# Retention attention and routed experts on one core: larger first pieces, constants by head pair, second buffers for two tiles

## The chip, the cores and the metric

The kernel runs on one core of a Trainium2 chip. The metric is device time in microseconds (us), the median of three runs. One further execution was profiled; every row below comes from it.

## The reference

```python
def _attn_ref(q, k, v):              # (8, 8, 576, 64) each
    scores = scale * np.matmul(q, k.transpose(0, 1, 3, 2))
    gamma = 1.0 - 2.0 ** (-5.0 - np.arange(H))
    Dmat = np.where(rel >= 0, gamma[:, None, None] ** rel, 0.0)
    return np.matmul(scores * Dmat, v)

def _moe_ref(x, w_gate, w1, w2):     # x: (4608, 512), 8 experts
    logits = x @ w_gate
    order = np.argsort(-logits.flatten())
    # greedy in this order: each token takes one expert,
    # each expert at most 576 tokens
    ...
    out[mask] = np.maximum(x[mask] @ w1[e], 0.0) @ w2[e]
```

The output of the attention, put together over heads, is the x of the expert part.

## The kernel before

The work has three parts, one behind the other: attention (to about 170 us), the routing search, and eight experts with a first layer (`ph`) and a second (`py`). The change touches attention alone.

Attention runs over 16 units. A unit `u` is a pair of batch entries with a pair of heads (`hp = u % 4`), and has nine blocks of 128 tokens. Four inputs are loaded per unit: `kin` and `qin` (transposed k and q, 1152 columns of fp32 on 128 partitions), `vin` (v by tokens, 1152) and `nin` (k by tokens, 1024). One block is numbered `g = 9*u + blk`. Its steps are these.

- `A(g)`: scores of the block on PE, two heads, into `pA` (line 588). Behind each fourth block VectorE multiplies by the decay mask and leaves `am` (line 593).
- `kscale2`: GpSimd (POOL) scales `nin` with constants into `ks` (line 568).
- `ST(u, c)`: the running state of k and v on PE into `pS` (line 605), which ScalarE scales into `S` (line 611).
- `XS` and `XW`: the block's output on PE, from the state (lines 628 and 630) and from `am` (line 640), into `pX`, a PSUM tile with two buffers. VectorE scales it into `xT` (line 652), which frees the `pX` buffer.
- `rows(bp, blk)`: VectorE transposes finished blocks of `xT` into `xr` (line 693). After every third block four DMAs write `xr` to DRAM as `xd` (line 698). `xr` has one buffer, so the first transpose of the next group waits until these writes are done.

Each engine works through its instructions in program order. All loads stand in one queue, that of SyncE (SP), in program order as well: a load whose buffer is still in use holds back every load behind it. `kin`, `qin` and `vin` have three buffers each, `nin` one. Loads of unit `u + 2` are issued while unit `u` runs (`ahead`).

The first two units are loaded in pieces. `fetch` takes a string: a lower-case letter with a number is a piece of unit 0, an upper-case one of unit 1; `c` and `h0`, `h1` are the constants. Before, unit 0 has three pieces per input (256, 256 and the remaining columns) and unit 1 two. The 3664 columns of constants lie by kind (`m1`, `m2`, `ex`, `ks`, `ss`), so that those of one head pair come in three transfers (line 532).

`warm(n)` issues n matmuls of a constant bf16 tile `full` into a PSUM tile that nothing reads. Before, it is called in the later parts only.

Of the kernel before, what the change touches and what calls it, by code (L numbers as in the profile page):

```python
# [10 lines left out]
F32 = mybir.dt.float32  # L11
F32R = mybir.dt.float32r
BF16 = mybir.dt.bfloat16
I32 = mybir.dt.int32
ALU = mybir.AluOpType
# [4 lines left out]
NP, HP, NB = 4, 4, 9  # L20
# [3 lines left out]
def consts_np():  # L24
    h = np.arange(H); g = (1.0 - 2.0 ** (-5.0 - h)).astype(np.float64)
    k = np.arange(128)[:, None, None]; q = np.arange(128)[None, None, :]
    gm = g[None, :, None]
    m1 = np.where(k <= q, gm ** (-k), 0.0)
    km = k % 64
    m2 = np.where((k // 64 == q // 64) & (k <= q), gm ** (-km), 0.0)  # L30
    m1 = np.broadcast_to(m1, (128, 8, 128)); m2 = np.broadcast_to(m2, (128, 8, 128))

    p = np.arange(128); gh = g.reshape(HP, 2)[:, p // 64].T
    i = np.arange(128)
    e1 = 0.125 * gh[:, :, None] ** i
    e2 = 0.125 * gh[:, :, None] ** (i % 64)
    ss = gh[:, :, None] ** (128.0 * np.arange(1, 5))
    c = np.arange(4)
    ks = g.reshape(HP, 1, 1, 2)[None] ** (-(128.0 * c[None, None, :, None, None] + p[:, None, None, None, None]))
    ks = np.broadcast_to(ks, (128, HP, 4, 2, 2))  # L40
    f = lambda a: np.ascontiguousarray(a, dtype=np.float32).reshape(128, -1)
    return np.concatenate([f(m1), f(m2), f(np.stack([e1, e1, e2], axis=2)), f(ks), f(ss)], axis=1)

def layout(q, k, v):

# [36 lines left out]
class Route:  # L82
# [9 lines left out]
    def fetch(s, nc, fc_d):  # L92
        s.nc = nc
        s.fc = s.pool.tile([128, fc_d.shape[1]], F32, name="rc_f")
        nc.sync.dma_start(s.fc, fc_d)
# [411 lines left out]

def attention(tc, nc, P, qk, vk, cst_d, wg_d, rf, xd, Lg):
    cst = P['c'].tile([128, 2*1024+3*512+64+16], F32, name="cst", tag="xg")
    W0 = cst.shape[1]  # L510
    m1 = cst[:, 0:1024].rearrange("p (h q) -> p h q", h=8)
    m2 = cst[:, 1024:2048].rearrange("p (h q) -> p h q", h=8)
    ex = cst[:, 2048:3584].rearrange("p (h j q) -> p h j q", h=4, j=3)
    ks = cst[:, 3584:3648].rearrange("p (h q) -> p h q", h=4)
    ss = cst[:, 3648:3664].rearrange("p (h q) -> p h q", h=4)
    wg = P['a'].tile([128, HP, 32], F32, name="wg")
    LD = {}
    def load(u, what, cuts=None):

        bp, hp = divmod(u, HP)  # L520
        for i in what:
            n = 1024 if i == "n" else 1152
            t = P['ld'].tile([128, n], F32, name=i + "in", bufs=dict(q=3, k=3, v=3, n=1)[i])
            src = qk[bp, hp, "qk".index(i)] if i in "qk" else vk[bp, hp, :, :1152] if i == "v" else vk[bp, hp, :, 1152:]
            LD[u, i] = t
            if cuts:
                pieces[u, i] = [(t[:, a:b], src[:, a:b]) for a, b in zip((0,) + cuts, cuts + (n,))]
            else:
                nc.sync.dma_start(t, src)
# [2 lines left out]
    part = lambda a, b: nc.sync.dma_start(cst[:, a:b], cst_d[:, a:b])  # L532

    def consts(hp):
        for a, n in ((0, 256), (2048, 384), (1024, 256)):
            if a or hp:
                part(a + n*hp, a + n*hp + n)
    load(0, "kqvn", (256, 512))
    load(1, "kqvn", (512,))

    def fetch(order):
        for x in order.split():
            if x == "c":
                part(0, 256)
                part(3584, 3664)
            elif x[0] == "h":
                consts(int(x[1]))
            else:
                nc.sync.dma_start(*pieces[x[0].isupper(), x[0].lower()].pop(0))
    fetch("k0 q0 c v0 n0 k1 q1 h0 n1 v1 k2 q2 n2 v2")  # L550
    NS = 4
    Sb = []
    for i in range(NS):
# [13 lines left out]
    def kscale2(u, a, b):  # L567
        nc.gpsimd.tensor_tensor(KS[u][:, a:b], LD[u, 'n'].rearrange("p (a d) -> p a d", d=64)[:, a:b],  # L568
                                ks[:, u % HP, a:b, None].to_broadcast([128, b-a, 64]), op=ALU.mult)
# [3 lines left out]
    def A(g):  # L573
        if g >= G: return
        u, blk = divmod(g, NB); hp = u % HP
        if blk == 0 and 2 <= u + 1 < 16:
            if u < 3:
                consts(u + 1)
            if u == 2:
                R.fetch(nc, rf)  # L580
                nc.sync.dma_start(wg[:, :, 0:8], wg_d.rearrange("(hp p) e -> p hp e", p=128))

        n, j, tail = (4, blk % 4, "") if blk < 8 else (1, 0, "t")
        if j == 0: PA[0] = [P['ps'].tile([128, n, 128], F32, name=f"pA{h}" + tail, tag="y" if tail else "h0", bufs=2) for h in range(2)]
        s = slice(blk*128, blk*128+128)
        for h in range(2):
            r = slice(64*h, 64*h+64)
            nc.tensor.matmul(PA[0][h][:, j], LD[u, 'k'][r, s], LD[u, 'q'][r, s], start=True, stop=True, skip_group_check=True)  # L588
        if j == n - 1:
            m = m2 if tail else m1  # L590
            for h in range(2):
                am = P['w'].tile([128, n, 128], F32, name=f"am{h}" + tail, bufs=2)
                nc.vector.tensor_tensor(am, PA[0][h], m[:, None, 2*hp+h, :].to_broadcast([128, n, 128]), op=ALU.mult)  # L593
                for i in range(n): AM[g-j+i, h] = am[:, i]
    def ST(u, c):

# [91 lines left out]
    def rows(bp, blk):  # L688

        j = blk % 3  # L690
        if j == 0:
            TR[0] = P['w'].tile([128, 12, HP, 32], F32, name="xr", bufs=1)
        nc.vector.transpose(TR[0][:, 4*j:4*j+4].rearrange("p b h i -> p h b i"),  # L693
                            XT[bp][:, :, blk*128:(blk+1)*128].rearrange("p h (b i) -> p h b i", i=32))
        if j == 2:
            o = (bp*NB + blk - 2)*128
            for a in range(4):
                nc.sync.dma_start(xd[o:o+384, 128*a:128*a+128].rearrange("(b j) c -> j b c", j=32),
                                  TR[0][32*a:32*a+32].rearrange("p b h i -> p b (h i)"))
# [70 lines left out]
        for n, (i, a, b) in enumerate(((1, 0, 1), (1, 1, 2), (2, 0, 2), (3, 0, 2), (4, 0, 2))):  # L770
            at(g0+24+2*n, R.first_table, i, 2*bp+a, 2*bp+b)
    kscale(0)
    kscale2(0, 0, 4)
    A(0)
    A(1)
    ST(0, 0)
    kscale2(0, 4, 8)
    kscale2(0, 8, 16)
    nc.gpsimd.memset(wg, 0.0)
    fetch("K0 Q0 N0 V0 h1 K1 Q1 N1 V1")  # L780
    A(2)
    A(3)

    def ahead(g):

# [306 lines left out]
def build(tc, nc, qk, vk, cst, wg, rf, w1, w2, out):  # L1092
    with ExitStack() as top:
        P = {}
        P['c'] = top.enter_context(tc.tile_pool(name="c", bufs=1))
        P['ps'] = top.enter_context(tc.tile_pool(name="ps", bufs=1, space=bass.MemoryType.PSUM))
        dr = top.enter_context(tc.tile_pool(name="dr", bufs=1, space=bass.MemoryType.DRAM))
        top.enter_context(tc.manual_schedule())
        xd = dr.tile([N, DM], F32, name="xd")
        it = P['c'].tile([128, 128], I32, name="it")  # L1100
        nc.gpsimd.iota(it, pattern=[[1, 128]], base=0, channel_multiplier=-1)
        P['ident_r'] = P['c'].tile([128, 128], F32R, name="ident")
        nc.vector.tensor_scalar(P['ident_r'], it, 0.0, None, op0=ALU.is_equal)
        P['ident'] = P['ident_r'].bitcast(F32)
        Lg = P['c'].tile([128, 36, 8], F32, name="Lg")
        mix = Mixer()
        full = P['c'].tile([128, 512], BF16, name="full")
        nc.vector.memset(full, 1.0)

        def warm(n):  # L1110

            ps = P['ps'].tile([128, DM], F32, name="warm", tag="y", bufs=2)
            for _ in range(n):
                nc.tensor.matmul(ps, full[:, :128], full, start=True, stop=True)
        P['warm'] = warm
        with ExitStack() as ctx:
            Q = dict(P)
            for name, bufs in (("a", 1), ("ld", 2), ("w", 2), ("xt", 2)):
                Q[name] = ctx.enter_context(tc.tile_pool(name="a_" + name, bufs=bufs))
            R, rows = attention(tc, nc, Q, qk, vk, cst, wg, rf, xd, Lg)  # L1120

            def idle(what):

                if what not in ("row", "rows"):
                    warm(what)
                    return
                for _ in range(1 + (what == "rows")):
                    if rows:
                        rows.pop(0)()
                    else:  # L1130
                        warm(1)
            R.idle = idle
            run = moe(tc, nc, P, R, xd, w1, w2, out, mix)
            mix.drain(lambda: 0 in run.regs)
            while rows:
                rows.pop(0)()
        P['w'] = top.enter_context(tc.tile_pool(name="w", bufs=1))
        run()
# [18 lines left out]
```

## Time and profile before

| what | us |
|---|---|
| median of three runs (lowest, highest) | 676.65 (674.9, 677.34) |
| the profiled execution | 674.55 |
| its span, first to last instruction | 672.8 |
| PE busy in the span | 632.0 (94%) |
| VectorE (DVE) busy | 422.3 (63%) |
| GpSimd (POOL) busy | 180.7 (27%) |

Busy shares are averages over three parts with different limits. What holds a part up is read from the waits and the chain of that part. Times within a trace count from the first instruction.

### The profile page before, as it was taken

The page shows a single profiled execution, that of the slowest core. Times are in us where ns is not written, and L with a number is a line of the kernel's source. Part 1 is how long each engine was busy: PE and PEld are TensorE (multiplying, and loading weights), DVE is VectorE, ACT ScalarE, POOL GpSimd, SP SyncE. Part 2 cuts the span into 40 slices and gives each one's busy share as a digit, 9 for nine tenths or more (in the row PEclk, how much of TensorE's full clock was granted, in tenths as well). Part 3 has the DMA queues.
Part 4 walks back from the last instruction along what each step waited for, and adds up shares of the span by engine and source line. Part 5 has one row for each costly group of instructions (what it writes and reads, how often), then busy time and mean ns, then how long its engine had stood idle before and what let it go on. Part 6 is the DMA issues. An engine that isn't in the chain of part 4 may idle for free.

```text
span 672.8 us, 14118 instructions
## 1 busy us (share of the span) xinstructions
PE 632.0 (94%) x5376; PEld 543.3 (81%) x5376; DVE 422.3 (63%) x1603; ACT 273.6 (41%) x488; POOL 180.7 (27%) x234
## 2 busy tenths in 40 slices
PE   4999999897987999999999999999999999999995
PEld 3887788776756887797798799889889989988984
DVE  2477878777775797798799599679776302211200
ACT  1333333232325524655257245515724643652611
POOL 2222212212212106315214323315224134131111
PEclk9999999899998999999999999999999999999998
DMA  7997999993455946978859938947894895894421
GB/s 225 340 362 251 285 306 307 257 282 91 126 198 137 227 96 203 258 192 199 247 130 230 243 81 215 245 145 172 210 245 118 177 268 177 194 237 137 94 63 39
DMA packets 53427, 134.72 MB, mean 200 GB/s; under 512 B 6128, under 2 KB 22512, under 8 KB 53360
## 3 DMA queue, kind: packets, MB, share of 16 engines
q1 hardware_dynamic: 38400, 81.91, 37.1%
q0 software_dynamic: 14960, 51.91, 35.1%
q8 instruction: 42, 0.69, 0.4%
q14 instruction: 25, 0.20, 0.1%
HBM read 81.90 MB, written 18.87 MB: 150 GB/s over the span
## 4 chain that ended last, share of the span: by engine, by line
PE 63%; DVE 12%; issue 9%; DMA 8%; POOL 3%; ACT 3%; SPq 2%; POOLq 0%; DVEq 0%; ACTq 0%
PE py L1037 21%; PE ph L998 21%; PE pX L640 4%; PE pA L588 3%; PE pX L630 3%; PE pS L605 3%; DMA w2l<-raw 2%; DMA raw<-in_w 1%; POOL xg L953 1%; DMA qin<-in_qk 1%; PE pt L969 1%; PE r L340 1%; DMA xd<-xr 1%; PE pT L669 1%; DVE xr L693 1%
## 5 line engine op out<-in xcount | busy, mean ns | idle before, releaser
L1037 PE MATMUL py<-w2h,hb 128*128 128x512 f32 x576 | 188.3, 399 | 0.0
L998 PE MATMUL ph<-xh,w1h 128*128 128x320 f32 (+1 forms) x512 | 152.6, 302 | 2.5 <-ACT xh L971 1.7
L998 PE MATMUL ph<-xh,w1l 128*128 128x320 f32 (+1 forms) x512 | 150.0, 297 | 0.0
L998 PE MATMUL ph<-xl,w1h 128*128 128x320 f32 (+1 forms) x512 | 149.9, 297 | 0.0
L1037 PE MATMUL py<-w2l,hb 128*128 128x512 f32 (+1 forms) x320 | 125.4, 392 | 0.1
L1037 PEld LDWEIGHTS py<-w2h,hb 128*128 128x128 f32 x576 | 104.0, 188 | 20.7
L998 PEld LDWEIGHTS ph<-xh,w1h 128*128 128x128 f32 x512 | 96.7, 190 | 4.7 <-ACT xh L971 2.8
L998 PEld LDWEIGHTS ph<-xl,w1h 128*128 128x128 f32 x512 | 96.9, 191 | 0.5 <-DVE cs L344 0.3
L998 PEld LDWEIGHTS ph<-xh,w1l 128*128 128x128 f32 x512 | 96.7, 191 | 0.2 <-DMA w1l<-raw 0.2
L1005 DVE SCALAR_TENSOR_TENSOR hb<-ph,hb 128x256 fp32r<-128x256 f32 (+1 forms) x192 | 58.9, 351 | 56.9 <-ACT hb L1002 56.2
L1002 ACT ACTIVATE hb<-ph 128x256 fp32r<-128x256 f32 (+1 forms) x128 | 52.2, 409 | 102.1 <-PE ph L998 102.1
L611 ACT ACTIVATE S<-pS,cst 64x128 f32<-64x128 f32 x128 | 46.4, 363 | 108.1 <-PE pS L605 106.5
L1014 POOL DMA_INDIRECT out_y<-yt,idx x40 | 40.8, 1021 | 118.8 <-ACT yt L1054 76.6
L1037 PEld LDWEIGHTS py<-w2l,hb 128*128 128x128 f32 (+1 forms) x320 | 56.7, 177 | 13.7 <-DMA w2l<-raw 1.0
L568 POOL TENSOR_TENSOR ks<-nin,cst 128x512 f32<-128x512 f32 (+1 forms) x33 | 33.3, 1028 | 120.8 <-DMA nin<-in_vk 100.9
L1054 ACT ACTIVATE yt<-py 128x512 f32<-128x512 f32 x32 | 19.2, 599 | 105.1 <-PE py L1037 78.9
L942 POOL DMA_DIRECT2D w2l<-raw x32 | 28.8, 901 | 119.2 <-ACT hb L1002 119.2
L593 DVE TENSOR_TENSOR am<-pA,cst 128x512 f32<-128x512 f32 x64 | 41.0, 682 | 27.9 <-PE pA L588 21.8
L953 POOL DMA_INDIRECT xg<-xd,idx x40 | 40.7, 1017 | 51.6 <-issue 26.6
L1057 DVE TENSOR_TENSOR yt<-yt,py 64x512 f32<-64x512 f32 x8 | 5.4, 678 | 69.6 <-ACT yt L1056 69.4
L588 PE MATMUL pA<-qin,kin 64*128 64x128 f32 x512 | 39.5, 295 | 8.6 <-DMA qin<-in_qk 8.6
L588 PEld LDWEIGHTS pA<-qin,kin 64*128 64x128 f32 x512 | 33.0, 196 | 12.8 <-issue 8.0
(190 smaller groups left out, 967.8 us busy)
## 6 DMA issues: line engine op xcount, KB each, us to landing
raw<-in_w SPq DMA_DIRECT2D x64, 512.0 KB, 5.3
w2l<-raw POOLq DMA_DIRECT2D x32, 512.0 KB, 5.7
w1l<-raw POOLq DMA_DIRECT2D x31, 512.0 KB, 7.7
kin<-in_qk SPq DMA_DIRECT2D x14, 576.0 KB, 6.3
qin<-in_qk SPq DMA_DIRECT2D x14, 576.0 KB, 7.1
vin<-in_vk SPq DMA_DIRECT2D x14, 576.0 KB, 7.9
nin<-in_vk SPq DMA_DIRECT2D x14, 512.0 KB, 5.8
xd<-xr SPq DMA_DIRECT2D x36, 192.0 KB, 3.6
```

The lines of the kernel that those rows point to most:

```text
L568: nc.gpsimd.tensor_tensor(KS[u][:, a:b], LD[u, 'n'].rearrange("p (a d) -> p a d", d=64)[:, a:b], ks[:, u % HP, a:b, None].to_broadcast([12 ...
L588: nc.tensor.matmul(PA[0][h][:, j], LD[u, 'k'][r, s], LD[u, 'q'][r, s], start=True, stop=True, skip_group_check=True)
L593: nc.vector.tensor_tensor(am, PA[0][h], m[:, None, 2*hp+h, :].to_broadcast([128, n, 128]), op=ALU.mult)
L611: nc.scalar.activation(st[64*h:64*h+64, :, 64*h:64*h+64], PS[u][64*h:64*h+64], AF.Copy, scale=ss[64*h:64*h+64, hp, c:c+1])
L640: nc.tensor.matmul(px[64*h:64*h+64, :], v[:, blk*128+64*h:blk*128+64*h+64], AM[g, h], start=False, stop=blk < 8, skip_group_check=True)
L942: nc.gpsimd.dma_start(lo, raw, accum_op=ALU.add)
L953: nc.gpsimd.indirect_dma_start(out=xg[:n, j, :], out_offset=None, in_=xd[:, :], in_offset=bass.IndirectOffsetOnAxis(ap=found[e][:n, j:j+1] ...
L998: T.matmul(ps, w, x, start=(k == 0), stop=(k == 11))
L1002: A.activation(hb[:, f, c], ps, AF.Relu)
L1005: V.scalar_tensor_tensor(hb[:, f, to+a:to+b], ps[:, a:b], 0.0, hb[:, f, 256*s+a:256*s+b].bitcast(F32), op0=ALU.max, op1=ALU.subtract)
L1014: st = nc.gpsimd.indirect_dma_start(out=out[:, :], out_offset=bass.IndirectOffsetOnAxis(ap=found[e][:n, t:t+1], axis=0), in_=y[:n], in_off ...
L1037: T.matmul(ps[:m], a, w, start=(k == 0), stop=(k == last), skip_group_check=True)
```

## The change

Units 0 and 1 both come in two pieces of 512 and the remaining columns. The first piece of q is issued from ScalarE's queue, all the others from SP's. Constants lie by head pair, so that a pair needs one transfer. All pieces of units 0 and 1 stand in one string ahead of the computation; the second string, which stood behind the first `kscale2` calls, is gone. `nin` and `xr` have two buffers each. The program begins with seven matmuls on `full`; `A(0)` to `A(3)` stand ahead of `ST(0, 0)`, and the first `kscale2` covers eight parts and not four.

```diff
-    load(0, "kqvn", (256, 512))
+    load(0, "kqvn", (512,))
     load(1, "kqvn", (512,))
...
-            t = P['ld'].tile([128, n], F32, name=i + "in", bufs=dict(q=3, k=3, v=3, n=1)[i])
+            t = P['ld'].tile([128, n], F32, name=i + "in", bufs=dict(q=3, k=3, v=3, n=2)[i])
...
     def consts(hp):
-        for a, n in ((0, 256), (2048, 384), (1024, 256)):
-            if a or hp:
-                part(a + n*hp, a + n*hp + n)
+        part(80 + 896*hp + (0 if hp else 256), 976 + 896*hp)
...
             if x == "c":
-                part(0, 256)
-                part(3584, 3664)
+                part(0, 336)
             elif x[0] == "h":
                 consts(int(x[1]))
             else:
-                nc.sync.dma_start(*pieces[x[0].isupper(), x[0].lower()].pop(0))
-    fetch("k0 q0 c v0 n0 k1 q1 h0 n1 v1 k2 q2 n2 v2")
+                (nc.scalar if x == "q0" else nc.sync).dma_start(*pieces[x[0].isupper(), x[0].lower()].pop(0))
+    fetch("k0 q0 c n0 v0 k1 q1 h0 n1 v1 K0 Q0 h1 N0 V0 K1 Q1 N1 V1")
...
-            TR[0] = P['w'].tile([128, 12, HP, 32], F32, name="xr", bufs=1)
+            TR[0] = P['w'].tile([128, 12, HP, 32], F32, name="xr", bufs=2)
...
     kscale(0)
-    kscale2(0, 0, 4)
-    A(0)
-    A(1)
+    kscale2(0, 0, 8)
+    P['warm'](7)
+    for g in range(4):
+        A(g)
     ST(0, 0)
-    kscale2(0, 4, 8)
     kscale2(0, 8, 16)
     nc.gpsimd.memset(wg, 0.0)
-    fetch("K0 Q0 N0 V0 h1 K1 Q1 N1 V1")
-    A(2)
-    A(3)
...
+        full = P['c'].tile([128, 512], BF16, name="full")
+        nc.vector.memset(full, 1.0)
         it = P['c'].tile([128, 128], I32, name="it")
...
-        full = P['c'].tile([128, 512], BF16, name="full")
-        nc.vector.memset(full, 1.0)
```

SP's queue before, from the third pieces of unit 0 on. The names are the tiles above, the numbers are partitions by columns, and the bracket names what the issue waits for (`Pool` is GpSimd, `DMAHW` an earlier load).

```order
L549 DMA kin<-in_qk 128x640 [waits DMAHW4_49]
L549 DMA qin<-in_qk 128x640 [waits DMAHW5_49]
L549 DMA nin<-in_vk 128x512 [waits DMAHW6_49]
L549 DMA vin<-in_vk 128x640 [waits DMAHW7_49]
L549 DMA kin<-in_qk 128x512 [waits DMAHW0_49]
L549 DMA qin<-in_qk 128x512 [waits DMAHW1_49]
L549 DMA nin<-in_vk 128x512 [waits DMAHW6_49,DMAHW2_49,Pool_49]
L549 DMA vin<-in_vk 128x512 [waits DMAHW3_49]
L532 DMA cst<-in_cst 128x256 [waits DMAHW4_49]
```

The seventh of these is the first piece of `nin` for unit 1; it waits for GpSimd. The same place of the queue in the changed kernel, from the second pieces of unit 0's `nin` and `vin` on:

```order
L545 DMA nin<-in_vk 128x512 [waits DMAHW0_49]
L545 DMA vin<-in_vk 128x640 [waits DMAHW1_49]
L545 DMA kin<-in_qk 128x512 [waits DMAHW2_49]
L545 DMA qin<-in_qk 128x512 [waits DMAHW3_49]
L531 DMA cst<-in_cst 128x896 [waits DMAHW4_49]
L545 DMA nin<-in_vk 128x512 [waits DMAHW5_49]
L545 DMA vin<-in_vk 128x512 [waits DMAHW6_49]
```

Unit 1's `nin` no longer waits for GpSimd, and the constants of its head pair are one transfer ahead of it.

PE's first instructions before, behind the branch at the start (`pA` with a number is the buffer of one head):

```order
L588 MATMUL pA_122<-qin,kin 128x128
L588 MATMUL pA_123<-qin,kin 128x128
L588 MATMUL pA_122<-qin,kin 128x128
L588 MATMUL pA_123<-qin,kin 128x128
L605 MATMUL pS<-vin,ks 64x64 x4
L588 MATMUL pA_122<-qin,kin 128x128
L588 MATMUL pA_123<-qin,kin 128x128
```

In the changed kernel, from the last of the seven matmuls on `full`:

```order
L1107 MATMUL warm<-full 128x512
L584 MATMUL pA_133<-qin,kin 128x128
L584 MATMUL pA_134<-qin,kin 128x128
L584 MATMUL pA_133<-qin,kin 128x128
L584 MATMUL pA_134<-qin,kin 128x128
L584 MATMUL pA_133<-qin,kin 128x128
L584 MATMUL pA_134<-qin,kin 128x128
L584 MATMUL pA_133<-qin,kin 128x128
L584 MATMUL pA_134<-qin,kin 128x128
L601 MATMUL pS<-vin,ks 64x64 x4
```

Four blocks of scores now stand ahead of the first state product, where two stood.

## Rows read from the trace of the kernel before

**Rows 1.** The page: the chain that ended last, share of the span by engine
```profile
PE 63%; DVE 12%; issue 9%; DMA 8%; POOL 3%; ACT 3%; SPq 2%; POOLq 0%; DVEq 0%; ACTq 0%
```
**Rows 2.** Stretches: length, busy time (and count) by engine, PE clock, DMA share, GB/s
```profile
0.00:3.40 3.40, 0.00 (x0) 0.00 (x0) 1.05 (x2) 0.00 (x0) 1.43 (x9) 1.00 0.40 102
3.40:12.60 9.20, 3.15 (x24) 2.45 (x25) 1.29 (x2) 2.01 (x3) 1.23 (x2) 1.00 0.89 263
12.60:18.96 6.36, 6.34 (x56) 5.79 (x56) 2.24 (x5) 0.72 (x2) 2.23 (x3) 1.00 0.75 248
18.96:27.34 8.38, 8.30 (x122) 7.25 (x120) 4.64 (x9) 2.90 (x8) 1.04 (x1) 1.00 0.97 359
28.36:74.00 45.64, 44.98 (x635) 37.73 (x636) 30.81 (x94) 15.35 (x42) 10.22 (x10) 1.00 0.89 306
150.00:164.00 14.00, 9.95 (x138) 8.44 (x134) 10.51 (x33) 2.90 (x8) 4.08 (x5) 1.00 0.49 134
164.00:170.00 6.00, 5.77 (x65) 4.24 (x65) 4.89 (x12) 2.18 (x6) 0.00 (x0) 0.72 0.08 15
```
**Rows 3.** Waits of PE, 0 to 165 us: total, times, longest
```profile
PE pA L588 <- DMA qin<-in_qk: 8.6, 4, 3.6
PE pX L630 <- DVE xT L652: 6.8, 4, 2.8
PE pS L605 <- POOL ks L568: 1.9, 1, 1.9
```
**Rows 4.** The chain that ended last, 0 to 33 us: start, length, what
```profile
7.36 5.80 DMA nin<-in_vk
...
14.67 0.43 SPq L549
...
19.22 9.01 DMA qin<-in_qk
28.36 1.16 PE pA L588 x16
...
32.17 0.45 PE pS L605 x8
```
**Rows 5.** Waits of SP's queue, 0 to 36 us
```profile
SPq L549 <- DMA nin<-in_vk: 3.5, 1, 3.5
...
SPq L549 <- POOL wg L779: 1.2, 1, 1.2
```
**Rows 6.** DMA totals of 2 to 14, 14 to 16 and 20 to 28 us
```profile
DMA packets 2506, 3.20 MB, mean 267 GB/s; under 512 B 405, under 2 KB 1776, under 8 KB 2506
...
DMA packets 125, 0.23 MB, mean 117 GB/s; under 512 B 11, under 2 KB 11, under 8 KB 125
...
DMA packets 924, 2.92 MB, mean 365 GB/s; under 512 B 102, under 2 KB 102, under 8 KB 923
```
**Rows 7.** POOL in order of time, 5 to 15 us: start, length, instruction, wait
```profile
5.95 0.61 POOL L568 TENSOR_TENSOR ks<-nin,cst 128x256 f32<-128x256 f32 x1 [3.86 <-DMA nin<-in_vk]
...
13.23 1.04 POOL L568 TENSOR_TENSOR ks<-nin,cst 128x512 f32<-128x512 f32 x1 [3.56 <-DMA nin<-in_vk]
```
**Rows 8.** Tile kin, 0 to 36 us: ns min/median/max, first and last start
```profile
L588 PE MATMUL pA<-qin,kin x96: 272/272/579, 3.5 to 34.0; 64*128 64x128 f32 x96
```
**Rows 9.** VectorE in order of time, 140 to 172 us
```profile
150.55 0.71 DVE L693 STREAM_TRANSPOSE xr<-xT 128x512 f32<-128x512 f32 x1 [1.35 <-DMA xd<-xr]
...
162.68 0.71 DVE L693 STREAM_TRANSPOSE xr<-xT 128x512 f32<-128x512 f32 x1 [2.02 <-DMA xd<-xr]
```
**Rows 10.** PE in order of time, 140 to 172 us
```profile
140.82 0.71 PE L630 MATMUL pX<-qin,S 128*128 128x128 f32 x4
...
152.32 0.49 PE L630 MATMUL pX<-qin,S 128*128 128x128 f32 x2 [1.39 <-DVE xT L652]
...
164.22 0.49 PE L630 MATMUL pX<-qin,S 128*128 128x128 f32 x2 [2.75 <-DVE xT L652]
...
166.82 1.20 PE L630 MATMUL pX<-qin,S 128*128 128x128 f32 x4
```

More of the change, by code (lines that the diff above doesn't have):

```diff
@@ L41, in consts_np @@
     f = lambda a: np.ascontiguousarray(a, dtype=np.float32).reshape(128, -1)
-    return np.concatenate([f(m1), f(m2), f(np.stack([e1, e1, e2], axis=2)), f(ks), f(ss)], axis=1)
+    ex = np.stack([e1, e1, e2], axis=2)
+    return np.concatenate([f(ks), f(ss)] + [f(a) for p in range(HP) for a in (m1[:, 2*p:2*p+2], ex[:, p], m2[:, 2*p:2*p+2])], axis=1)
 def layout(q, k, v):
@@ L509, in attention @@
     cst = P['c'].tile([128, 2*1024+3*512+64+16], F32, name="cst", tag="xg")
[L510 to L515, printed above, removed]
+    ks = cst[:, 0:64].rearrange("p (h q) -> p h q", h=4)
+    ss = cst[:, 64:80].rearrange("p (h q) -> p h q", h=4)
+    cq = cst[:, 80:].rearrange("p (h j q) -> p h j q", h=4, j=7)
+    m1, ex, m2 = cq[:, :, 0:2], cq[:, :, 2:5], cq[:, :, 5:7]
     wg = P['a'].tile([128, HP, 32], F32, name="wg")
@@ L589, in A @@
         if j == n - 1:
-            m = m2 if tail else m1
+            m = (m2 if tail else m1)[:, hp]
             for h in range(2):
                 am = P['w'].tile([128, n, 128], F32, name=f"am{h}" + tail, bufs=2)
-                nc.vector.tensor_tensor(am, PA[0][h], m[:, None, 2*hp+h, :].to_broadcast([128, n, 128]), op=ALU.mult)
+                nc.vector.tensor_tensor(am, PA[0][h], m[:, None, h, :].to_broadcast([128, n, 128]), op=ALU.mult)
                 for i in range(n): AM[g-j+i, h] = am[:, i]
```

## Prediction

> **What bounds the kernel now.** I read the page first. PE has 63% of the chain that ended last and DMA 8% [rows 1], so the loads bind only somewhere. The table by stretch says where. PE is busy 3.15 of the 9.20 us to 12.60, and from 28.36 to 74 it is busy 44.98 of 45.64 us [rows 2]. The start waits, the middle does not.
>
> The waits name two things. PE waited 8.6 us for `qin` and 6.8 us for VectorE's `xT` up to 165 us [rows 3]. The chain shows the first as one path: a piece of `nin`, an issue on SP, the load of unit 2's q issued at 19.22 and landed 9.01 us later, and then PE's scores at 28.36 [rows 4]. Everything before 28.36 is set by how fast the first units arrive, with PE close behind: from 12.60 to 27.34 it is hardly idle [rows 2].
>
> The second is in VectorE's own order. Its transposes at 150.55 and 162.68 waited 1.35 and 2.02 us until the earlier `xr` had been written out [rows 9], and PE, whose `pX` buffers VectorE frees, stood 1.39 and 2.75 us [rows 10]. Those are 4.1 of the 6.8 us; the other two waits are shorter.
>
> **The change: the start.** What unit 2's scores need is the same before and after: units 0 and 1 at 2.294 MB each (three inputs of 1152 columns and one of 1024, 512 bytes a column) and 0.958 MB of constants, together 5.55 MB, then k and q of unit 2, 1.18 MB. I count at what rate they arrive.
>
> Up to 3.40 us the rate was 102 GB/s, 0.35 MB [rows 2]; at 267 GB/s that is 1.3 us, so the flow begins at 2.1. From 2 to 14 us it was 267 GB/s, when 1776 of 2506 packets were under 2 KB; from 20 to 28 us, with 102 of 924 under 2 KB, 365 GB/s [rows 6]. Between them there is a hole: SP stood 3.5 and 1.2 us for `nin` and what GpSimd did with it [rows 5], and from 14 to 16 us only 0.23 MB came in where 267 GB/s gives 0.53, which costs 0.30 / 0.267 = 1.1 us.
>
> Before by this count: 2.1 + 5.55/0.267 (20.8) + 1.18/0.365 (3.2) + 1.1 = 27.2. The trace has 28.2 (19.22 + 9.01) [rows 4]. The 1.0 us left over I keep as lag.
>
> After: the second `nin` buffer takes the hole away. Pieces are now 2 KB a row or more (512 columns and up; only `c` has 1344 bytes). Their rate lies between 267 and 365 GB/s; I take 300, nearer to the lower end because 2 KB is nearer to what ran there. That gives 2.1 + 18.5 + 3.2 + 1.0 = 24.8, which is 3.5 us before 28.36. Bounds: at 267 GB/s 27.1 (gain 1.2), at 365 GB/s 21.5 (gain 6.8).
>
> Next in line is unit 2's `nin`. The state product that needs it ran at 32.17 [rows 4], 3.81 us behind the scores. After, v and n, 1.11 MB at 365, land 3.05 us behind q, at 27.9, and GpSimd takes 1.04 [rows 7]: 28.9, where PE is there at 28.7. So 0.2 us are given back: **gain 3.3 us** (1.0 to 6.6).
>
> Can PE follow? Its work from 12.60 to 27.34 is 6.34 us in which the matmuls ran slowly, and 8.30 us. In the rows of `kin` one shape takes 272 ns and up to 579 [rows 8]; the long ones are those before 18.96, where the clock column reads 1.00 all the same. I read them as the lower level, 1.2 GHz, and what follows as 2.4. At 2.4 GHz the work is 6.34/2 + 8.30 = 11.5 us. After, the last piece of unit 0's q has landed when 1.88 MB are in, at about 9. With the same 6.4 us at the lower level PE is through at 9 + 6.4 + 8.3 = 23.7, a little ahead of 24.8.
>
> From 28.36 to 74 the loads flowed at 306 GB/s at a share of 0.89, and PE was idle for 0.66 of 45.64 us [rows 2]. The whole stretch moves forward, loads and PE alike; I cost that at nothing. If the loads don't move with it, it costs the 3.3.
>
> **Edits at nothing.** The seven matmuls on `full` run where PE had nothing (0 of the first 3.40 us [rows 2]). If they last longer than the first q takes, they delay scores whose state product waits for `ks` anyway. That product now needs eight parts scaled, 1.04 us and not 0.61 [rows 7]: 0.4 later, hidden since the next scores wait for q until 9. Eight constant transfers fewer save SP 8 × 0.43 us [rows 4], and q's first piece on ScalarE 0.43 more, but SP is ahead of the data, so nothing. The identity made 0.5 us later is used tens of us on.
>
> **The change: `xr`.** With two buffers a group's first transpose waits for the writes of the group before the last, long done. VectorE gets 1.35 + 2.02 = 3.4 us back, and PE's waits shrink by as much, from 4.1 to 0.8. Bounds: 4.1 if all of PE's wait goes; 2.0 if VectorE's own work ahead of `xT` keeps it late at the first place. **Gain 3.4 us.**
>
> Behind the second stall the granted clock was 0.72 in the mean from 164 to 170 us, a part of it at 1.2 GHz: four products took 1.20 us there and 0.71 at 140.82 [rows 2, 10]. PE had stood 2.75 us before. The loss is at most 0.28 × 6 = 1.7 us. With 0.8 us of standing left I expect it gone in the main; part of it VectorE would take up (4.89 busy of 6 us [rows 2]), so **gain 1.2 us** (0 to 1.7).
>
> **Sum.** 3.3 + 3.4 + 1.2 = 7.9 us. The profiled execution took 674.55 (span 672.8 and 1.75 around it), so it would be 666.7. It is 2.1 below the median of the runs; from 676.65 the same gain gives **668.7**.
>
> **The rivals.** *Larger pieces do not flow faster*, only the hole closes: the start gains 1.0, the total 1.0 + 4.6 = 5.6, 671.1. For it: at 12.60 to 18.96 mixed pieces ran no faster, 248 GB/s with the hole [rows 2]. Against it: 267 and 365 GB/s by packet size [rows 6]. The Trainium skill, DMA: Bandwidth & Descriptors, Specifications, says that a transfer reaches line rate from 512 B on; by that rule 1 KB rows lose nothing and this rival holds. The trace so far leans against it, though it can't part packet size from time.
>
> *The start's gain is given back*: PE, earlier by 3.3 us, meets loads of units 3 and 4 that are not earlier, because the flow is already at a share of 0.89 [rows 2]. Total 4.6, 672.0. Against it: those loads follow in the same queue, without the hole.
>
> *The `xr` wait is replaced*: the freed VectorE time ahead of `xT` goes into another wait of the same length, for `pX` or the scores. Only the start is left, 3.3 us, 673.3. Against it: nothing else is named in VectorE's wait at either place [rows 9].
>
> *Slower: PE's clock stays low.* The pieces come evenly and PE takes them in small bites with waits between, where before it had one long stretch from 12.60. My sum has 1.2 GHz until about 15.4. Each further us at it costs 0.5. All of the 7.9 is eaten after 15.8 us more, at 31; beyond 0.5% slower (another 3.4) it must last until 38, and until 40 it gives 676.65 + 12.3 - 7.9 = 681. Against it: once PE falls behind the loads it no longer waits, and before, 6.4 us of that sufficed [rows 2]. The Trainium skill, TensorE: Matmul & The Clock Gate, What's actually happening, says that the throttled level is the default and activity releases it; the long durations at the start agree [rows 8], and by that rule the seven first matmuls may bring the rise forward, which I don't count.
>
> **How the numbers follow.** About 0.5% (3.4 us) is what a measurement of this kernel can tell from no change. Forecast 0.55; larger pieces no faster 0.2; start given back 0.1; `xr` replaced 0.08; slower 0.05; 0.02 for more gain than the bounds. The forecast, larger pieces no faster, three quarters of the start given back, and the last are faster: 0.85. The other quarter and `xr` replaced are within 0.5%: 0.11. Slower 0.04, as a low clock can also end within the band. Bounds of the terms: 1.0 + 2.0 + 0 = 3.0 to 6.6 + 4.1 + 1.7 = 12.4, 673.6 to 664.3. The range 664 to 673 leaves out the slower case, most of the `xr` rival and what lies beyond the bounds.
>
> **What would show it.** Right: unit 2's scores begin at 24 to 26 us, SP issues unit 1's `nin` without GpSimd, the flow from 2 to 14 us is near 300 GB/s with no hole, VectorE has no wait for `xd<-xr`, PE's waits for `xT` sum to about 3.5 us, and the clock stays at 1.00 behind the last of them. Wrong: a flow of 267 (first rival), new waits for `qin` between 28 and 74 us (second), 1.39 and 2.75 us still there (third), or scores at 579 ns past 20 us (the slower one).

## The result, and the profile after

The changed kernel took 667.34 us (median of 4 runs, 665.16 to 667.43), the kernel before 676.43 beside it (4 runs, 674.9 to 677.34). The ratio is 0.986, with an interval of 0.9833 to 0.9887, so the gain is 9.1 us by the medians. The profiled execution took 667.28 us, its span is 665.5. Line numbers of the changed kernel are 4 lower than those of before in attention (`pA` is line 584, `pX` 626, `xr` 689).

The page, chain that ended last, share of the span by engine. The DMA share fell from 8% [rows 1] to 6%:

```profile
PE 66%; DVE 13%; issue 10%; DMA 6%; ACT 2%; POOL 2%; SPq 0%; POOLq 0%; DVEq 0%; ACTq 0%
```

The chain from 0 to 30 us (start, length, what) and the DMA totals of 2 to 14 and of 20 to 28 us:

```profile
0.75 3.50 DMA qin<-in_qk
...
6.37 6.78 DMA cst<-in_cst
...
13.17 8.81 DMA qin<-in_qk
...
22.11 1.16 PE pA L584 x16
...
24.36 0.41 PE pS L601 x8
...
24.85 1.05 POOL ks L564
...
25.95 0.45 PE pS L601 x8
```

```profile
DMA packets 2236, 4.50 MB, mean 375 GB/s; under 512 B 242, under 2 KB 370, under 8 KB 2236
...
DMA packets 849, 3.27 MB, mean 408 GB/s; under 512 B 95, under 2 KB 95, under 8 KB 848
```

Unit 2's scores begin at 22.11 instead of 28.36, and its state product at 25.95 instead of 32.17 [rows 4]. The load of unit 2's q takes as long as before (8.81 and 9.01 us), but it is issued at 13.17 instead of 19.22. The flow was 375 GB/s where it had been 267, and 408 where it had been 365 [rows 6].

PE's waits up to 165 us (total, times, longest), and the stretches (length, busy time and count of PE, PEld, VectorE, ScalarE and GpSimd, PE clock, DMA share, GB/s):

```profile
PE pX L626 <- DVE xT L648: 2.4, 3, 1.1
PE pA L584 <- DMA qin<-in_qk: 1.6, 2, 1.3
...
PE pS L601 <- POOL ks L564: 0.5, 2, 0.3
```

```profile
8.00:10.00 2.00, 1.51 (x20) 1.49 (x20) 0.22 (x1) 1.25 (x3) 0.10 (x1) 0.84 1.02 382
10.00:12.00 2.00, 2.00 (x17) 1.60 (x16) 1.47 (x4) 0.00 (x0) 1.09 (x2) 0.50 1.05 410
...
155.00:160.00 5.00, 4.05 (x52) 2.80 (x52) 3.50 (x9) 1.96 (x6) 0.00 (x0) 1.00 0.32 56
...
195.00:200.00 5.00, 5.00 (x26) 4.27 (x24) 1.12 (x2) 1.98 (x4) 0.00 (x0) 0.50 0.02 7
```

PE's wait for `qin` shrank from 8.6 to 1.6 us and that for `xT` from 6.8 to 2.4 [rows 3]. VectorE has no wait for `xd<-xr` at all; the transpose that had waited 2.02 us [rows 9] now runs without one:

```profile
151.72 0.71 DVE L689 STREAM_TRANSPOSE xr<-xT 128x512 f32<-128x512 f32 x1
```

PE ran at 1.2 GHz (clock 0.50) from about 9.4 to 12.8 us and again behind the gather of the first expert, from about 194 to 204 us. Behind the place of the last wait for `xr`, from 155 to 160 us, the clock is 1.00, where it was 0.72 in the mean before [rows 2].

I read the same six places in every profile. The table gives when each begins, in us; "search" is the first 36 products of the routing search, "expert 0" its first layer.

| kernel | unit 2's scores | unit 9's scores | search | expert 0 | its second layer | span |
|---|---|---|---|---|---|---|
| before | 28.36 | 93.20 | 181.24 | 207.38 | 240.37 | 672.8 |
| after | 22.11 | 87.59 | 169.28 | 195.59 | 229.91 | 665.5 |
| one `xr` buffer | 24.53 | 89.99 | 177.94 | 203.72 | 236.95 | 670.1 |
| `xr` alone | 26.99 | 91.75 | 174.01 | 200.93 | 235.13 | 667.8 |
| hole alone | 26.26 | 90.71 | 177.00 | 202.89 | 235.96 | 671.7 |
| small pieces | 24.91 | 90.31 | 172.93 | 198.93 | 233.99 | 667.8 |
| the change once more | 22.02 | 87.94 | 172.02 | 198.30 | 231.13 | 666.1 |

Against before, the changed kernel is 6.25 us ahead at unit 2, 5.61 at unit 9, 11.96 at the search, 11.79 at expert 0, 10.46 at its second layer, and 7.3 at the end. In this execution what is won is won in attention, and some is lost behind it.

### The profile page after: what moved, and what is told of

The parts are those of the page before. It is cut to its first block, busy times and chain, and to the rows that moved or that the text cites. A ratio compares the mean times of both kernels' runs of the same rounds, so it can differ in the third digit from the quotient of the medians.

```text
span 665.5 us, 14105 instructions
## 1 busy us (share of the span) xinstructions
PE 633.5 (95%) x5381; PEld 542.3 (81%) x5383; DVE 420.1 (63%) x1603; ACT 273.1 (41%) x488; POOL 180.7 (27%) x233
## 4 chain that ended last, share of the span: by engine, by line
PE 66%; DVE 13%; issue 10%; DMA 6%; ACT 2%; POOL 2%; SPq 0%; POOLq 0%; DVEq 0%; ACTq 0%
PE py L1030 24%; PE ph L991 20%; PE pA L584 4%; PE pX L636 4%; PE pX L626 3%; PE pS L601 3%; DMA qin<-in_qk 2%; PE pt L962 2%; DMA raw<-in_w 2%; PE r L341 2%; PE pT L665 1%; DVE G L168 1%; PE pX L624 1%; DMA cst<-in_cst 1%; DMA w2l<-raw 1%
## 5 line engine op out<-in xcount | busy, mean ns | idle before, releaser
L564 POOL TENSOR_TENSOR ks<-nin,cst 128x512 f32<-128x512 f32 x32 | 33.3, 1058 | 113.7 <-DMA nin<-in_vk 102.4
L589 DVE TENSOR_TENSOR am<-pA,cst 128x512 f32<-128x512 f32 x64 | 41.1, 683 | 22.1 <-PE pA L584 15.6
L935 POOL DMA_DIRECT2D w1l<-raw x31 | 27.7, 907 | 59.4 <-ACT w1l L934 36.8
```

The costliest lines, as they stand in the source:

```text
L589: nc.vector.tensor_tensor(am, PA[0][h], m[:, None, h, :].to_broadcast([128, n, 128]), op=ALU.mult)
L935: nc.gpsimd.dma_start(lo, raw, accum_op=ALU.add)
```

## The experiments

My theory was that the start (flow and hole) and the second `xr` buffer are two separate gains of about the same size. The rivals were that only one of them counts, and that at the start something other than the larger pieces does it. The kernel before ran beside each of them on the same chip, with medians of 673.04, 677.16 and 675.05 us on the three chips, so kernels are compared by the ratio to it, not by the time.

**One `xr` buffer in the changed kernel.**

```
-TR[0] = P['w'].tile([128, 12, HP, 32], F32, name="xr", bufs=2)
+TR[0] = P['w'].tile([128, 12, HP, 32], F32, name="xr", bufs=1)
```

> The changed kernel with one xr buffer again; all else as changed. Theory (the second xr buffer gives VectorE its two waits back, and PE with it): unit 2's scores stay at 22.1 us, VectorE waits again twice for xd<-xr, some 3.4 us together, PE's waits for xT rise from 2.4 to about 6 us, the routing search starts 4 to 6 us later than 169.3, and the time is 671 to 673. Rival (the xr wait was only the name of a longer VectorE chain): the waits come back but PE's hardly grow, and the time stays at 667 to 668.

Measured: 669.89 us, ratio 0.9953 (0.9926 to 0.998). Its waits up to 172 us, VectorE's and PE's, and the stretches from 10 to 12 and from 158 to 166 us:

```profile
DVE xr L689 <- DMA xd<-xr: 4.8, 4, 2.7
```

```profile
PE pX L626 <- DVE xT L648: 6.8, 4, 3.9
PE pS L601 <- DMA vin<-in_vk: 2.9, 1, 2.9
```

```profile
10.00:12.00 2.00, 1.43 (x13) 1.46 (x15) 0.00 (x0) 1.68 (x3) 0.00 (x0) 0.50 1.05 403
...
158.00:166.00 8.00, 5.89 (x59) 5.15 (x59) 5.66 (x13) 1.81 (x5) 0.00 (x0) 0.57 0.00 0
```

VectorE waits at both places of before again, 0.6 and 2.7 us, and at two more; PE's waits are back at 6.8 us. Behind the longest of them, 3.9 us, the clock is low again (0.57 in the mean). What is left of the gain, 0.47% or 3.2 us (1.3 to 5.0), is the start's. The loads came as in the changed kernel (403 GB/s here), yet unit 2's scores did not stay at 22.1 us but began 2.4 us later: PE waited 2.9 us once for `vin`, and was at 1.2 GHz from 8.6 to 15.4 us. How much of the start is gained so depends on PE too, and differs between executions.

**`xr` alone in the kernel before.** The same line of before with `bufs=2`.

> The kernel before with a second xr buffer and nothing else. Theory: unit 2's scores stay at 28.4 us, no VectorE wait for xd<-xr, the search starts 4 to 6 us before 181.2, and the time is 671 to 673. Rival (the second buffer only helps once the start is earlier): the time stays at 675.5 to 677.

Measured: 668.82 us, ratio 0.9937 (0.9913 to 0.996), 4.2 us (2.7 to 5.9). PE's wait up to 165 us, and the search's first products in the chains of before, of this kernel and of the changed one:

```profile
PE pX L630 <- DVE xT L652: 3.2, 3, 1.2
```

```profile
181.24 1.48 PE r L290 x36
```

```profile
174.01 1.48 PE r L290 x36
```

```profile
169.28 1.48 PE r L291 x36
```

From unit 9 to the search it takes 82.26 us, the changed kernel 81.69, before 88.04. VectorE has no wait for `xd<-xr`. The search comes 7.2 us earlier than before, where 4 to 6 were expected. Of the two gains each counts: 0.47% and 0.63% make 1.10%, the whole change has 1.4% (1.13 to 1.67). The intervals of the two leave room for the rest; that they add up to the whole is not shown. Its start is untouched, and yet unit 2's scores began 1.4 us earlier than in the profile of before. So much one execution differs from another there, and of the 6.25 us at unit 2 some 4.9 are left if this profile is the base.

**Without the seven first matmuls**, twice, on two chips, the second time beside the unaltered changed kernel.

```
-    P['warm'](7)
```

> The changed kernel without the seven matmuls on the constant tile. Theory (the flow of the loads sets the start, the matmuls run in idle time and add nothing): unit 2's scores within 0.5 us of 22.1, the time 666.5 to 668. Rival (the seven matmuls bring the clock's rise forward, and PE would otherwise lag behind the loads): 1.2 GHz until 13 us or later without a break before, unit 2's scores at 23.5 or later, and the time 668.5 to 670.

> The changed kernel without its seven first matmuls, a second time and beside the changed kernel itself. Theory (they bring nothing: unit 2's scores were at 23.2 without and at 22.1 to 24.9 with them): time within 0.2% of the changed kernel's on this chip. Rival (they help where the clock's phase is kind): 0.3% or more slower than it.

> The changed kernel once more, beside the other two. Theory (start and xr buffer as in its first profile): unit 2's scores at 22 to 25 us as the clock falls, no wait for xd<-xr, the search at 169 to 172, the time 0.983 to 0.989 of the kernel before. Rival (the first profile was a lucky one): ratio 0.990 or more.

Measured: 663.41 us, ratio 0.9844 (0.9794 to 0.9894), and 667.27 us, 0.9884 (0.9856 to 0.9912). The changed kernel once more: 667.45 us, 0.9887 (0.9842 to 0.9932). Unit 2's scores began at 23.16, 22.73 and 22.02 us. The seven matmuls are worth nothing that the time shows, though the scores came 0.6 to 1.1 us later without them. By the durations of its products (417 ns, later 272) PE was at 1.2 GHz up to 13 or 14 us without them. In the eight profiles with them the fast level came at 4.2 to 6.1 us, as the prediction held possible; but in six of the eight the clock fell to 1.2 GHz again between 7.6 and 9.5 us, and rose at 12.8 to 16.3 us. In the profile of the changed kernel once more PE's wait for `xT` is 5.2 us:

```profile
PE pX L626 <- DVE xT L648: 5.2, 3, 2.4
```

There is no wait for `xr` in it, so VectorE's own work can still make `xT` late, in some executions more than in others. The 2.4 us of it stand at 116.5 us, where no wait for `xr` had been in before.

**Small pieces in the changed kernel**: the cut of before, all else as changed.

```
-    load(0, "kqvn", (512,))
+    load(0, "kqvn", (256, 512))
-    fetch("k0 q0 c n0 v0 k1 q1 h0 n1 v1 K0 Q0 h1 N0 V0 K1 Q1 N1 V1")
+    fetch("k0 q0 c n0 v0 k1 q1 h0 n1 v1 k2 q2 n2 v2 K0 Q0 h1 N0 V0 K1 Q1 N1 V1")
```

> The changed kernel with unit 0 in three pieces again (256, 256 and the remaining columns); constants by head pair, two nin buffers and the rest stay. Theory (rows of 2 KB and more flow faster): the flow from 2 to 8 us falls from about 360 to 270 GB/s and unit 2's scores start at 24 to 25 us, the time is 669 to 670. Rival (the hole and the many constant transfers held the flow down): scores still at 22 to 23 us and the time 667 to 668.

Measured: 666.86 us, ratio 0.9884 (0.9828 to 0.994), below the 669 to 670 expected; scores at 24.91, as expected. The DMA totals of 2 to 14 and of 4 to 6 us, and SP in order of time:

```profile
DMA packets 2547, 3.99 MB, mean 333 GB/s; under 512 B 275, under 2 KB 1409, under 8 KB 2547
...
DMA packets 552, 0.58 MB, mean 292 GB/s; under 512 B 59, under 2 KB 501, under 8 KB 552
```

```profile
4.04 0.43 SPq L545 DMA_DIRECT2D nin<-in_vk  x1
4.51 0.43 SPq L545 DMA_DIRECT2D vin<-in_vk  x1
4.99 0.43 SPq L545 DMA_DIRECT2D kin<-in_qk  x1
5.46 0.43 SPq L545 DMA_DIRECT2D qin<-in_qk  x1
```

SP issues one transfer per 0.475 us. A piece of 256 columns is 131,072 bytes, so SP can start 276 GB/s of these and no more (ScalarE adds one piece, and the constants go in larger ones). The flow was 244, 292 and 316 GB/s in the three stretches of 2 us up to 8 us. Later, with larger transfers in the queue, it was 368 and more, as in the changed kernel. The scores' delay is not the flow's alone: PE did not wait for unit 2's q, and was at 1.2 GHz from 9.1 to 15.9 us. The price in whole time is too small for this measurement.

**The hole alone**: the kernel before with a second `nin` buffer and nothing else.

```
-bufs=dict(q=3, k=3, v=3, n=1)
+bufs=dict(q=3, k=3, v=3, n=2)
```

> The kernel before with a second nin buffer and nothing else. Theory (the hole is worth little; the small pieces hold the flow down by themselves): no hole at 14 to 16 us, the flow from 2 to 12 us stays at 210 to 290 GB/s, unit 2's scores at 27 to 27.5 us (28.4 and 27.0 in the two profiles with one buffer), the time within 0.3% of the kernel before. Rival (with the hole gone the queue stays full and the flow rises by itself): 340 GB/s or more from 12 us on and unit 2's scores at 25 or earlier.

Measured: 674.25 us, ratio 0.9965 (0.9937 to 0.9992); scores at 26.26. Its chain at the start, with SP's issues one behind the other, and its totals of 2 to 14 and 14 to 22 us; then the total of 14 to 22 us of the kernel before:

```profile
5.47 0.43 SPq L549
...
5.94 0.43 SPq L549
...
6.41 0.43 SPq L549
...
6.89 5.40 DMA qin<-in_qk
...
12.42 2.08 PE pA L588 x16
```

```profile
DMA packets 2556, 3.29 MB, mean 274 GB/s; under 512 B 408, under 2 KB 1792, under 8 KB 2556
...
DMA packets 1543, 3.26 MB, mean 408 GB/s; under 512 B 167, under 2 KB 551, under 8 KB 1542
```

```profile
DMA packets 1205, 2.02 MB, mean 253 GB/s; under 512 B 131, under 2 KB 515, under 8 KB 1205
```

SP stands in its chain from 0.76 to 6.84 us with 0.04 to 0.06 us between its issues, so up to there these are the limit: by 6.4 us it had issued pieces of 1.55 MB, and by 8 us 1.43 MB had come. From 12 us on the flow was as the rival had it, 392 GB/s and more, while the scores lie between the two. Behind 14 us the same pieces flow at 408 GB/s instead of 253. The hole had cost 155 GB/s over 8 us, 1.24 MB or 3.0 us of loading at 408 GB/s, where I had counted 1.1. Yet the scores came only 2.1 us earlier than in before's profile, 0.7 than in that of `xr` alone, and the time gained 0.35%. The chain says why: unit 0's last q landed only at 12.3 us (6.89 + 5.40; the changed kernel's products with it begin at 8.49), and from 12.42 to 30 us the chain is PE's alone. PE was then behind, and no load stands in the chain any more. So closing the hole is worth little until the pieces ahead of it come faster too.

**The constants in smaller parts**: the changed kernel with three transfers per head pair, as before.

```
-        part(80 + 896*hp + (0 if hp else 256), 976 + 896*hp)
+        o = 80 + 896*hp
+        for a, b in ((0, 256), (256, 640), (640, 896)):
+            if a or hp: part(o + a, o + b)
```

> The changed kernel with the constants of each head pair in three transfers (256, 384 and 256 columns; two for the first) and not one. Theory (rows of 1 to 1.5 KB cost flow only where they are issued): 330 to 380 GB/s from 6 to 14 us and 390 or more elsewhere; unit 2's scores at 22 to 25 as the clock allows. Rival (the number of transfers in the queue, not the row, holds the flow down): under 330 GB/s over the whole of 4 to 20 us.

Measured, in one run: 668.59 us; scores at 22.87. The totals of 2 to 14 and of 10 to 12 us:

```profile
DMA packets 2633, 4.42 MB, mean 368 GB/s; under 512 B 286, under 2 KB 1054, under 8 KB 2633
...
DMA packets 550, 0.77 MB, mean 386 GB/s; under 512 B 59, under 2 KB 346, under 8 KB 550
```

1054 packets are under 2 KB instead of 370, and the flow is 368 instead of 375 GB/s. In a stretch where 346 of 550 are, it is 386. From 6 to 14 us it was 380 to 388, so the rival does not hold. In this run rows of 1 to 1.5 KB do not slow the flow where the issues are not what limits it.

**Small pieces from two issuing engines**: the small pieces again, with all of unit 0's q and v issued by ScalarE.

```
-(nc.scalar if x == "q0" else nc.sync)
+(nc.scalar if x in ("q0", "v0", "q1", "v1", "q2", "v2") else nc.sync)
```

> The changed kernel with unit 0 in three pieces, as in the run with small pieces, but every piece of q and v of unit 0 issued from ScalarE and the others from SP, so that two engines issue. In the run with small pieces alone the flow was 292 and 316 GB/s from 4 to 8 us; one engine issued 128 KB each 0.47 us, which is 277 GB/s. Theory (SP's issue rate holds the small pieces down): 350 GB/s or more from 4 to 8 us. Rival (the 1 KB rows themselves are slow): still 290 to 320 GB/s.

Measured, in one run: 669.29 us; scores at 25.56. The total of 4 to 6 us, PE's longest wait up to 36 us, and a later stretch:

```profile
DMA packets 616, 0.72 MB, mean 362 GB/s; under 512 B 67, under 2 KB 511, under 8 KB 616
```

```profile
PE pS L601 <- POOL ks L564: 4.2, 1, 4.2
```

```profile
14.00:16.00 2.00, 2.00 (x18) 1.71 (x18) 1.43 (x4) 0.00 (x0) 0.66 (x1) 0.50 0.95 334
```

511 of 616 packets are the small rows, and they came at 362 GB/s where they had come at 292 with 501 of 552. Who issues them differs, and with it the order between the two queues; so the issues were the limit. The scores came no earlier all the same. PE waited 4.2 us, up to 11.00, for the first `ks`, since the pieces of `nin` came later (1.8 us, up to 8.92, with one issuing engine). From 10 to 16 us the flow fell to between 318 and 346 GB/s, which I cannot explain, and PE was at 1.2 GHz up to 16 us. The Trainium skill, DMA: Bandwidth & Descriptors, Issuing engines are not separate DMA queues, says that issuing from several engines only saves the time on the sequencer, usually small. The trace agrees with the first half (362 against 292 GB/s); here that time, 0.475 us per 128 KB, was not small but the limit.

**Six matmuls in PE's gap**, behind the first state product.

```
     ST(0, 0)
+    P['warm'](6)
```

> The changed kernel with six more matmuls on the constant tile behind the first state product, where PE waits for unit 0's second q piece. Theory (with the flow at 390 GB/s the start is bound by PE's clock, which fell to 1.2 GHz at about 9 us in each run that had the seven matmuls): no fall at 9 us, unit 2's scores at 20 to 22 us against 22.1, 24.5 and 24.9, the time 0.2 to 0.4% below the changed kernel's. Rival (the loads bind at 22 anyway): the clock holds but PE waits for unit 2's q, scores at 22 or later, and the time as the changed kernel's.

Measured: 666.6 us, ratio 0.9852 (0.9795 to 0.9909). PE in order of time, and the stretch from 10 to 12 us:

```profile
7.52 1.47 PE L1108 MATMUL warm<-full 128*128 128x512 bf16 x6
...
21.96 1.16 PE L584 MATMUL pA<-qin,kin 64*128 64x128 f32 x16 [0.65 <-DMA qin<-in_qk]
```

```profile
10.00:12.00 2.00, 2.00 (x34) 1.72 (x31) 1.68 (x4) 0.54 (x2) 1.19 (x2) 1.00 1.06 407
```

The clock stays at 2.4 GHz where the changed kernel's profile fell to 1.2 (0.50 in its row of 10 to 12 us). That the six matmuls hold it is not shown by this, since the changed kernel once more stayed at 2.4 GHz without them. With the clock up PE is ahead and waits 0.65 us for unit 2's q, and the scores begin at 21.96 instead of 22.11. In the changed kernel once more it waits 1.4 us there. So with the clock up the loads are what binds at 22 us, and a faster PE brings nothing more. The time, expected 0.2 to 0.4% lower by the theory, can't tell that from no change.

**More matmuls while the first gather is waited for**, 11 instead of 3, in the changed kernel.

```
         next(tr)
-        warm(3)
+        warm(11)
```

> The changed kernel with eleven matmuls on the constant tile where three stood, behind the first transposes of expert 0, where PE waits 2.1 us for the second gathered tile. Theory (of the gain at the search, 12.0 us in the profiles, 1.3 is lost to PE's clock, which fell to 1.2 GHz for 10.2 us there): PE holds 2.4 GHz through expert 0's first layer, from whose start to the first product of its second layer it takes 32 us or less (34.3 in the changed kernel's profile, 33.0 before), and the time is 1 to 2 us below the changed kernel's of the same chip. Rival (the loss lies in the weights' loads): still 33 us or more, no gain.

Measured: 665.19 us, ratio 0.985 (0.9819 to 0.988), beside 0.9887 (0.9842 to 0.9932) of the changed kernel on the same chip. PE in order of time, and the stretch behind:

```profile
192.97 2.55 PE L1107 MATMUL warm<-full 128*128 128x512 bf16 x11
...
196.49 0.74 PE L991 MATMUL ph<-xh,w1h 128*128 128x256 f32 x4 [0.24 <-ACT xh L964]
```

```profile
195.00:200.00 5.00, 4.76 (x40) 3.97 (x39) 1.91 (x5) 2.37 (x4) 0.15 (x1) 1.00 0.27 80
```

The clock stays at 1.00 there, and expert 0's first layer takes 32.04 us (196.49 to 228.53) instead of 34.32. Each of the other twelve profiles has a stretch at 1.2 GHz behind the gather, of 3.4 to 10.2 us; the changed kernel once more, with 3.4 us of it, took 32.83. So the low clock there can be taken away, for 0.8 us beside that profile. The intervals of the two ratios overlap, so the time does not prove a faster kernel.

## Why the prediction was right, and what was off

668.7 us was forecast, 667.34 came; 7.9 us of gain against 9.1 (7.6 to 11.3 by the interval). The sign and the two sources are right. The terms are not all of their size, and one rests on a wait that was not there. Of the signs named, VectorE's waits for `xd<-xr`, unit 1's `nin` and the clock behind the last group came as said; the flow (375 GB/s, not near 300) and the scores (22.11, not 24 to 26) did not.

**The start was mis-sized, in the flow.** The step "I take 300" GB/s from 2 to 14 us measured 375, above the 365 that I had set as the upper bound, and the flow behind it 408 instead of 365. The sum with these two is 2.1 + 5.55/0.375 (14.8) + 1.18/0.408 (2.9) + 1.0 = 20.8, and the last piece landed at 13.17 + 8.81 = 21.98. The scores came 4.9 to 6.3 us earlier by the profiles, where 3.3 was forecast, near the upper bound of 6.6. In whole time the start is worth 3.2 us (1.3 to 5.0) by the run with one `xr` buffer, so there the size of the term stays open.

The reason I gave for a rate between 267 and 365, rows under 2 KB, is wrong in the main: from 4 to 6 us rows of mostly 1 KB came at 362 GB/s with two issuing engines, the changed kernel's at 391. Two other things held the flow. SP's issues did up to about 8 us, 0.475 us each for mostly 128 KB: 208 to 259 GB/s in the kernel before and in the hole alone, 294 to 391 after, and at equal rows 292 with one issuing engine and 362 with two. The hole did from 14 to 22 us, with its 3.0 us instead of 1.1. Between them, from 8 to 12 us, the hole alone had only 216 and 332 GB/s with rows of mostly 2 KB; what held it there stays open, as it does for two issuing engines from 10 to 16 us. I had put "SP is ahead of the data" beside the edits at nothing; the chain of the hole alone shows the opposite. So does the chain of before, which rows 4 show from 7.36 us on only: from 0.76 to 7.31 us it is one issue of SP behind the other, and again from 14.42 to 19.17.

```profile
0.76 0.39 SPq L549
...
6.88 0.43 SPq L549
```

The first rival, that rows of 1 KB lose nothing, had the better reason and the wrong outcome, since larger pieces also need fewer issues. The Trainium skill, DMA: Bandwidth & Descriptors, Specifications, has transfers at line rate from 512 B on. The 362 and 386 GB/s, with rows of mostly 1 KB and more, agree with it.

**What was given back** at unit 2's `nin` was 0.2 us by the forecast and 0.03 by the profiles: the state product stands 3.84 us behind the scores (25.95 and 22.11) where it stood 3.81 before. GpSimd's `ks` at 24.85 is in the chain, but what released it was PE's state product at 24.36 and not the load of `nin`. So it was before:

```profile
30.61 0.41 PE pS L605 x8
...
31.07 1.05 POOL ks L568
```

The step left this wait for PE out. The load it had nearly right: in the profile of the change once more `nin` landed 2.7 us behind q, where 3.05 was forecast, and 0.16 us ahead of GpSimd's start.

**The `xr` term is right.** 3.4 and 1.2 us for the clock make 4.6; by the time of `xr` alone it is 4.2 (2.7 to 5.9). From unit 9 to the search the two profiles differ by 6.35 us, but a part of that is the execution of before: it had a stretch at 1.2 GHz that I had overlooked,

```profile
119.00:125.00 6.00, 4.32 (x47) 3.84 (x49) 4.46 (x17) 1.29 (x4) 2.05 (x2) 0.72 0.94 224
```

and the two other profiles with one `xr` buffer do not have it; they took 1.5 and 1.8 us less from unit 9 to unit 12, the changed kernel 1.9. What is left is 4.4. From unit 12 to the search the three profiles with one buffer take 56.59 to 58.54 us and the ten with two 52.39 to 53.15. The term for the clock is borne out as well: at or behind the last wait for `xr` each of the three has a stretch at 1.2 GHz, and from 145 to 172 us none of the ten.

**The edits at nothing** cost nothing that the profile shows: PE's first state product, with eight parts scaled, begins at 6.71 us and its next scores wait for q up to 8.49, as foreseen. The seven matmuls bring nothing either, as the two runs without them show. The fewer issues of SP do not belong here, as said above; what they bring by themselves was not run.

**What I did not foresee** lies behind attention. The first expert's first layer took 34.32 us instead of 32.99, 1.3 lost to the low clock behind the gather: 10.2 us of it where before had 3.4. That is this execution's, since the changed kernel once more had 3.4 and took 32.83. And in expert 4 (counted from 0) 2.9 us more are lost: its first layer took 31.49 us instead of 28.57. PE's waits there, of the changed kernel and of before:

```profile
PE r L341 <- DVE G L168: 2.6, 2, 1.5
```

```profile
PE r L340 <- DVE G L167: 1.1, 1, 1.1
```

The same 2.9 us stand in 8 of the 12 profiles taken after that of before, the hole alone among them, which is nearly the kernel before. So this is not the change's doing. It goes with the chip: of the twelve the four taken on one chip, the runs with one `xr` buffer, `xr` alone, small pieces and the first without the seven matmuls, do not have it, and all seven taken on two others do (for the first profile of the change and that of before the chip is not on record). Why it does stays open. It would explain why the profiled gain of 7.3 us at the end is smaller than 9.1 by the medians.

**The rivals.** The start's gain was not given back: 5.61 of 6.25 us are there at unit 9. The `xr` wait was not replaced: at its two places PE had stood 4.1 us, and in the ten profiles with two buffers it stands there 0.6 to 1.3 (0.8 forecast). Of all its waits for `xT` 2.4 us are left, 3.5 forecast, and the 5.2 us of the other execution show how far VectorE's own work moves that. The slower case did not come; its mechanism is real, but small. In the runs with one `xr` buffer, small pieces and two issuing engines PE was at 1.2 GHz between 8 and 16 us, and the scores were 2.4 to 3.5 us later than 22.11; in those with smaller constants and with more matmuls at the gather it was so too, and they were 0.8 and 1.2 us later. It was never low up to 31 us, the point from which it would have decided.

## What to carry to other kernels

Before a slow flow is put down to row size, count how long the issuing engine takes per transfer: bytes per transfer over its issue interval is an upper bound of the flow, and with small first pieces it can be the limit. A wait in the middle of an issue queue can cost more than the hole that it leaves in the flow: here the flow stood at 117 GB/s for 2 us, but was low for 8. That the requests behind it had run out is my reading of that, not shown by itself. And where a kernel's gain is a few us, read the same landmarks in several profiles: two executions of code that is the same up to there differed by 1.4 us at the start, and one expert by 2.9 us from chip to chip.

## What was not expected of the hardware

- SP's issues of 0.43 us, 0.475 apart, held the loads of mostly 128 KB to 208 to 259 GB/s up to 8 us. With mostly 256 KB and more per transfer the same queue reached 375 to 410 GB/s.
- Closing a hole of 2 us raised the flow of the 8 us from 14 on from 253 to 408 GB/s, by one profile of each.
- The clock at the start differs between executions of one code: PE was busy for 0.82 of the 2 us from 6 to 8, and the clock fell to 1.2 GHz at 9.4; once more it was busy for 0.83, and the clock did not fall. The scores of unit 2 began at 22.11 and 22.02 us.
